# Mode rows in two-byte parts, a later start of gating, and moved norms, taps and restores in a four-layer kernel of long convolutions

## The chip, the cores and the metric

The kernel runs on one core of one Trainium2 chip. A core has TensorE (PE, matrix products), VectorE (DVE), ScalarE (ACT), GpSimd (POOL) and a queue that issues transfers (SP, SyncE); POOL can issue transfers too. Each engine works through its own list of instructions in order and waits on semaphores for the others. The metric is the time of one execution on the device in microseconds, as the median of several runs.

## The reference

Four layers, A, B, A, B, each added to its input. The input x is `q`, 2048 positions by 512 channels.

```python
def A(q, k, v, shift_k, ssm_k, ssm_D):        # q is layernorm(x)
    k_shift = short causal convolution of k with 4 taps per channel
    kv = k_shift * v
    y = irfft(rfft(kv, 4096) * rfft(ssm_k, 4096))[:2048] + kv * ssm_D
    return q * y

def B(u, log_A_real, A_imag, C_real, C_imag, log_dt, D_skip):   # u is layernorm(x)
    dt = exp(log_dt);  A = -exp(log_A_real) + 1j * A_imag;  C = (C_real + 1j * C_imag) * dt
    K = 2 * einsum("dn,dnl->dl", C, exp(A * dt * l)).real       # 128 modes per channel, l = 0..2047
    y = irfft(rfft(K, 4096) * rfft(u, 4096))[:2048]
    return y + u * D_skip

x = q
x = x + A(layernorm(x));  x = x + B(layernorm(x))
x = x + A(layernorm(x));  x = x + B(layernorm(x))
```

In A only the factor `q` depends on x; in B the kernel K does not. So the convolution of A and the spectrum of K are the same in both rounds.

## The kernel before

**Convolutions.** The 512 channels go in 4 quarters of 128, a transform of 4096 points in two steps of matrix products: `fwd_group` multiplies by a table (L171, `pf<-u,wz` or `pf<-kk,wz`) and VectorE transposes the result (L189, L191); `f2_chunk` (L196, `pu<-…,w2`) makes one of 8 chunks of a quarter's spectrum. For a kernel's spectrum (`spectrum_quarter`) four loads `kk` come (L229), POOL adds D to the first tap (L239), and the chunks are copied by ScalarE (`pc`, L247) and stored to `spec` (L248). In `convolution` a chunk is multiplied by the stored spectrum `kab`: ScalarE swaps real and imaginary part (`sw`, L281, L282), VectorE multiplies `vv` (L283), POOL multiplies `sw` (L285) and adds (L286, every third one on VectorE in B). The way back is L295 (`pi<-vv,mm`), a copy (L296), a transpose (`w`, L310) and L316 (`po<-w,w4`); then `finish` takes `po` away.

**Taps of B.** The exponents of the modes are made on four tiles of 128 by 512 (`la`, `ai`, `ph`, `t2`): decay, turns per step, and phase and log magnitude of C. `split` (L359 to L366) parts each into a high and a low four-byte half (`hl`, cast L362 and subtraction L363) and writes both, transposed, to `rows_d`. From there `load_rows` fetches the rows of 32 channels (`raw`, L470), 16 times in all, and VectorE casts them to the matmul's four-byte form (`rw`, L472). Each `rw` gives 10 matmuls against small tables of steps: `mags` (L479, `pm`, 6 of them, then an exponential on ScalarE, L485) and `angles` (L494, `pa`, 4 of them). For an angle VectorE rounds to whole turns (`y`, L498) and a second matmul (L499, table `minus`) subtracts them in the same bank. `waves` takes sine and cosine (L505 to L507), `products` multiplies them on POOL and VectorE (`xye`, L517 to L521), `contract` (L531) sums over the modes, and the taps go to `kdram` (L543), whence `spectrum_quarter(1, q)` loads them as `kk`.

**Gating of A.** `gated(grp)` makes `kv` for 32 channels, 16 groups in all: a load (L624), four multiplies by taps on POOL (L629), a copy on ScalarE (L635), three additions and a product on VectorE (L637, L639), a store (L640). `kv_steps` goes through the groups in three steps each.

**What sets the order.** The code asks for the work in steps, and two generators take turns: `stream` (taps, 64 steps, and B's spectra after each quarter) and `diagonal` (A's spectra in 48 steps, gating, then A's convolution), one step of the first to two of the second; four steps of `diagonal` go ahead of all. A scheduler then puts each engine's list in order by its own estimates; `after(a, b)` gives it an order between two instructions that needs no wait. The first layer follows: `gated_update` loads A's result (`yaq`, L723) and x (L720) and updates x, with statistics; `conv_b(0)` is the second layer, in which the norms `u` of a quarter (`norm`, L798 to L815) run on the engines that `NORM1`, `NORMQ` name; then `gated_update` and `conv_b(1)` for the second round. In the second round x is changed back by `restore` (L818 to L820, 16 additions of `off` on VectorE), asked for at the third quarter's start. Buffers come from named pools; a buffer's `bufs` says how many there are.

Of the kernel before, what the change touches and what calls it, by code (L numbers as in the profile page):

```python
# [11 lines left out]
F16 = mybir.dt.float16  # L12
# [8 lines left out]
NQ = 4  # L21
# [58 lines left out]
def mode_constants():  # L80
    m = np.arange(32)
    n2 = np.concatenate([32 + m, 31 - m])
    tabs = {
        "tt": (np.concatenate([m + 1, 64 * m + 32]), np.repeat([0, 1], 32)),
        "tg1": (n2, 0 * n2),
        "tg2": (64 * m, 0 * m + 1),
    }
    out = {}
    for name, (rate, off) in tabs.items():
        t = np.zeros((2, 2, 16, 2, 16, len(rate)), np.float32)  # L90
        for ch in range(16):
            t[:, 0, ch, :, ch] = rate
            t[:, 1, ch, :, ch] = off
        out[name] = t.reshape(128, 16, len(rate))
    out["minus"] = -np.eye(128, dtype=np.float32)
    return out
# [3 lines left out]
def kernel(ctx: ExitStack, tc: tile.TileContext, out, x_in, kv_in, ssmk_in, ssmd_in,  # L100
# [18 lines left out]
    rows_d = [dram.tile([NQ, 128, 4, 128], F32, name=f"rows_d{k}") for k in range(2)]  # L119
# [23 lines left out]
    psum, swapped, turned, added = {}, [None], [None], [None]  # L143
# [29 lines left out]
    def fwd_group(src, z, c0, n, step, first=None, tag="c1", full=True, early=None):  # L173
        for j in range(0, n, step):
# [12 lines left out]
            if step == 32:  # L187
                for r in range(2):
                    turned[0] = V.transpose(zr[:, :, r], pf[..., r].rearrange("p a x t -> p x a t"))  # L189
# [33 lines left out]
    def spectrum_quarter(which, q, src, pool, zlast, zb, tag):  # L223
# [3 lines left out]
        for g in range(4):  # L227
            kk = pool.tile([128, 512], F32, name="kk", tag="kk", bufs=3 - which)
            nc.sync.dma_start(kk, src[4 * q + g])  # L229
# [12 lines left out]
        for c in range(NCH):  # L242
# [3 lines left out]
            pc = pool.tile([128, CK * 128], F32, name="pc", tag="pc", bufs=2)  # L246
            S.copy(pc, pu.rearrange("p k c -> p (k c)"))  # L247
# [5 lines left out]
    def convolution(which, pools, steps, finish, lag, ahead, nk, ns, nw, inplace, add_dve, zlast=None, late_step=None, first_b=False):  # L253
# [18 lines left out]
        for s in range(-2 * NCH, NS + lag + NCH + 1):  # L272
# [3 lines left out]
            if 0 <= s < NS:  # L276
# [6 lines left out]
                V.tensor_mul(vv, pu, kabs[s][:, 0])  # L283
# [73 lines left out]


    def split(i, v, eng):  # L359
        k, r = divmod(i, 2)  # L360
        hl = nat.tile([128, 2, 4, 128], F32R, name="hl", tag="hl", bufs=4)
        S.copy(hl[:, 0], v)  # L362
        eng.tensor_sub(hl[:, 1], v, hl[:, 0])  # L363
        nc.sync.dma_start(rows_d[k].rearrange("q (h r x) g n -> r (q h) x (g n)", h=2, r=2)[r]
                          .rearrange("a (c p) y -> a c (p y)", p=2),
                          hl.rearrange("p s g n -> p (s g n)").bitcast(F32))  # L366
# [52 lines left out]
    for key, w_, src in (("tg2", 32, tg2_in), ("tg1", 64, tg1_in), ("tt", 64, tt_in)):  # L419
        tabs[key] = gp.tile([128, 16, w_], F32R, name=key)  # L420
# [38 lines left out]

    rows, ms, pks, angs = {}, {}, {}, {}  # L460
# [3 lines left out]
    def load_rows(gi):  # L464
        if gi in rows:
            return
        raw = wk.tile([128, 2, 128], F32, name="raw", tag="raw", bufs=2)
        q, g = divmod(gi, 4)
        for k in range(2):
            nc.sync.dma_start(raw[:, k, :], rows_d[k][q, :, g, :])  # L470
        rows[gi] = wk.tile([128, 2, 128], F32R, name="rw", tag="rw", bufs=2)
        V.tensor_copy(rows[gi], raw)  # L472

    def mags(gi, k, col):
        h, s = divmod(k, 2)
        hs = slice(64 * h, 64 * h + 64)
        pm = pp.tile([128, 512], F32, name="pm", tag="pa", bufs=NPA)
        rhs = tabs["tg2"][hs] if col == 2 else tabs["tg1"][hs, 8 * s:8 * s + 8, :]
        mt = T.matmul(pm, rows[gi][hs, 1, :], rhs, start=True, stop=True)  # L479
# [10 lines left out]
    def angles(gi, k):  # L490
        h, s = divmod(k, 2)
        hs = slice(64 * h, 64 * h + 64)
        pa = pp.tile([128, 512], F32, name="pa", tag="pa", bufs=NPA)
        T.matmul(pa, rows[gi][hs, 0, :], tabs["tt"][hs, 8 * s:8 * s + 8, :], start=True, stop=False,  # L494
# [116 lines left out]
    with ExitStack() as actx:  # L611
# [31 lines left out]
        KV0 = 1  # L643
# [35 lines left out]
        def diagonal():  # L679
            kvs = kv_steps()  # L680
            for q in range(NQ):
                for i, _ in enumerate(spectrum_quarter(0, q, ssmk_in, ap, zlast, ZA, "c1")):
                    if q == 0 and i == 1:
                        for grp in range(KV0):
                            for _ in gated(grp):
                                pass
# [14 lines left out]
            yield from convolution(0, {"conv": ap}, steps_a, finish_a, lag=LAGA, ahead=AHA, nk=NKA, ns=NSA, nw=NWA, inplace=True,  # L701
# [262 lines left out]
```

## Time and profile before

| | us |
|---|---|
| median of 3 runs (739.62 to 749.3) | 739.74 |
| profiled execution, whole | 734.99 |
| profiled execution, span | 733.2 |
| busy in the span: PE, DVE, ACT, POOL | 593.9, 531.1, 486.0, 454.8 |

The profiled execution is 4.75 us below the median; all times of single instructions are from it. Its mean granted TensorE clock is 0.933 of full speed. The stages on its time axis: preparation of the modes to about 45 us, with A's first spectra beside it; taps, spectra and A's convolution to about 422; the first layer's update to 455; the second layer with the last spectra of B to about 595; the third layer to about 616; the fourth to the end. In rows of the timeline the columns are start, length, engine, line, operation, output and inputs, count, and in brackets how long the engine was idle before and what released it; in rows of groups the busy time and the mean duration in ns stand behind the bar, then the idle time ahead of the group.

### The profile page before, as it was taken

Reading aid. Unit: us, or ns where it says so; the run is one execution under the profiler, and the core shown is the slowest. Engines: PE = TensorE matmul, PEld = TensorE weight load, DVE = VectorE, ACT = ScalarE, POOL = GpSimd, SP = SyncE. Lnnn points to the kernel's source line nnn. Section 1 sums busy time; section 2 is a strip of 40 time slices with the busy share of each in tenths; the row PEclk is TensorE's granted clock in tenths of the full one; section 3 lists DMA queues with packets and bytes.
Section 4 is the critical chain, followed back from the end, with each engine's and each line's share of the span. In section 5 each row is a group of like instructions: output and inputs, shape, how many; then the busy total and the mean of one; then the engine's idle time right before and its main releaser. Section 6 shows DMA issues by size and latency. Waiting matters only on the chain. (4 is left out here: it accounts for less than half of the span.)

```text
span 733.2 us, 14282 instructions
## 1 busy us (share of the span) xinstructions
PE 593.9 (81%) x4984; PEld 409.9 (56%) x4984; DVE 531.1 (72%) x961; ACT 486.0 (66%) x882; POOL 454.8 (62%) x473
## 2 busy tenths in 40 slices
PE   1378877698989999969998865899798817799996
PEld 0154554456766776736765454767476503476773
DVE  7857959877385785584574877376597998978775
ACT  4246566577678777776798749677655447768672
POOL 5847969678268595684596620157576612479693
PEclk9997979768999999989999996999999978899999
DMA  9769767774745457636457493567866360178682
GB/s 324 258 227 315 255 209 235 226 249 158 223 125 143 130 127 204 167 107 173 118 149 212 136 335 150 170 181 203 226 192 164 85 172 0 51 209 238 195 244 100
DMA packets 80683, 135.39 MB, mean 185 GB/s; under 512 B 8540, under 2 KB 29412, under 8 KB 79460
## 3 DMA queue, kind: packets, MB, share of 16 engines
q1 hardware_dynamic: 79716, 132.06, 60.3%
q0 software_dynamic: 896, 2.43, 1.2%
q8 instruction: 39, 0.64, 0.4%
q14 instruction: 32, 0.26, 0.1%
HBM read 98.80 MB, written 35.65 MB: 183 GB/s over the span
## 5 line engine op out<-in xcount | busy, mean ns | idle before, releaser
L285 POOL TENSOR_TENSOR sw<-sw,kab 128x512 f32<-128x512 f32 x96 | 124.9, 1305 | 66.3 <-ACT sw L282 61.3
L283 DVE TENSOR_TENSOR vv<-pu,kab 128x512 f32<-128x512 f32 x96 | 65.1, 680 | 64.1 <-ACT sw L282 44.1
L295 PE MATMUL pi<-vv,mm 128*128 128x128 f32 x768 | 105.7, 281 | 6.7 <-DVE vv L283 4.3
L286 POOL TENSOR_TENSOR vv<-vv,sw 128x512 f32<-128x512 f32 x76 | 98.6, 1301 | 14.5 <-DVE vv L283 12.0
L295 PEld LDWEIGHTS pi<-vv,mm 128*128 128x128 f32 x768 | 94.2, 193 | 20.6 <-issue 10.4
L281 ACT ACTIVATE sw<-pu 64x512 f32<-64x512 f32 x96 | 57.1, 595 | 65.7 <-PE pu L196 61.8
L171 PE MATMUL pf<-kk,wz 128*128 128x256 f32 (+1 forms) x176 | 64.7, 624 | 42.1 <-issue 15.2
L517 POOL TENSOR_TENSOR xye<-co,m 128x512 f32<-128x512 f32 x64 | 76.0, 1187 | 36.5 <-ACT co L507 12.5
L629 POOL TENSOR_TENSOR term<-kvt 128x512 f32<-128x512 f32 x64 | 81.5, 1292 | 19.5 <-ACT acc L635 9.8
L196 PEld LDWEIGHTS pu<-zu,w 128*128 128x128 f32 x512 | 63.0, 191 | 42.8 <-DVE vv L283 16.1
L196 PE MATMUL pu<-x,w 128*128 128x128 f32 x512 | 79.6, 302 | 5.9 <-ACT pc L247 2.5
L196 PEld LDWEIGHTS pu<-x,w 128*128 128x128 f32 x512 | 70.7, 209 | 21.9 <-issue 7.5
L196 PE MATMUL pu<-zu,w 128*128 128x128 f32 x512 | 72.8, 284 | 10.7 <-DVE vv L283 9.6
L171 PE MATMUL pf<-u,wz 128*128 128x256 f32 (+2 forms) x280 | 76.4, 485 | 3.0 <-DVE zu L189 1.2
L247 ACT COPY pc<-pu 128x512 f32<-128x512 f32 x64 | 37.2, 587 | 45.3 <-PE pu L196 22.6
L485 ACT ACTIVATE m<-pm 128x512 f32<-128x512 f32 x96 | 53.4, 607 | 18.5 <-PE pm L479 15.1
L316 PE MATMUL po<-w,w 128*64 128x512 f32 x192 | 53.9, 637 | 13.8 <-DVE w L310 12.0
L171 PEld LDWEIGHTS pf<-kk,wz 128*128 128x128 f32 (+1 forms) x176 | 30.1, 222 | 58.2 <-issue 29.3
L505 ACT ACTIVATE co<-pa 128x512 f32<-128x512 f32 x64 | 38.4, 600 | 30.2 <-PE pa L499 29.8
L282 ACT COPY sw<-pu 64x512 f32<-64x512 f32 x96 | 55.5, 578 | 1.1
L518 DVE TENSOR_TENSOR xye<-pa,m 128x512 f32<-128x512 f32 x64 | 43.7, 683 | 13.8 <-ACT pa L506 7.3
L479 PE MATMUL pm<-tg,rw 64*128 64x512 f32 x96 | 43.7, 517 | 10.5 <-DVE xye L519 8.3
(137 smaller groups left out, 1147.3 us busy)
## 6 DMA issues: line engine op xcount, KB each, us to landing
kab<-spec SPq DMA_DIRECT2D x188, 256.0 KB, 4.3
spec<-pc SPq DMA_DIRECT2D x64, 256.0 KB, 2.3
kvt<-kv_in SPq DMA_DIRECT2D x16, 624.0 KB, 5.3
yaq<-ya_d SPq DMA_DIRECT2D x5, 1024.0 KB, 7.5
kk<-ssmk_in SPq DMA_DIRECT2D x16, 256.0 KB, 5.1
kv_d<-un SPq DMA_DIRECT2D x16, 256.0 KB, 4.1
xt<-x_in SPq DMA_DIRECT2D x16, 256.0 KB, 2.9
kdram<-ks SPq DMA_DIRECT2D x64, 64.0 KB, 2.9
```

The source lines that it names most:

```text
L171: yield T.matmul(o, w, rhs, start=True, stop=True)
L196: ins = T.matmul(pu[:, i, :], w2[:, c * CK + i, :], z[:, :, c * CK + i, :], start=True, stop=True)
L281: S.mul(sw[0:64], pu[64:128], -1.0)
L282: swapped[0] = S.copy(sw[64:128], pu[0:64])
L283: V.tensor_mul(vv, pu, kabs[s][:, 0])
L285: (V if last else G).tensor_mul(sw, sw, kabs[s][:, 1])
L286: (V if last or s % add_dve == add_dve - 1 else G).tensor_add(vv, vv, sw)
L295: i1s[t] = T.matmul(pi[:, i, :], mm[:, c * CK + i, :], vvs[t][:, i, :], start=True, stop=True)
L316: ins = T.matmul(po[64 * a:64 * a + 64], w4, ws[g][:, :, 16 * a:16 * a + 16, :].rearrange("p x t r -> p t x r"), start=True, stop=True, ti ...
L485: i = S.activation(m, pm.rearrange("p (c i) -> p c i", c=16 if col == 2 else 8), AF.Exp)
L517: G.tensor_mul(xye[:, 0, :, 32:96], co[:, :, 1:65], m[:, :, 32:96])
L629: G.tensor_mul(term, kvt[:, 3 - j:19 - j, :], tap(j))
```

## The change

1. **Mode rows.** `split` makes three two-byte parts, each the rounded rest of what is left, and a fourth part of zeros, so that the 128 partitions of `rw` hold 2 halves of the channels, 2 kinds of rows, 8 channels and 4 parts. That is one more cast on ScalarE and one more subtraction per tile (POOL for `la` and `ai`, VectorE for `ph` and `t2`). `rows_d` holds bf16, `load_rows` loads straight into `rw` (3 buffers), the cast is gone. The tables `tt`, `tg1`, `tg2` are bf16. L479 and L494 become two-byte matmuls over 64 rows (128 for the second kind of magnitudes) with the same 512 columns. The subtraction of whole turns (L499) keeps its four-byte form.
2. **Gating.** No group is done ahead (`KV0` 1 to 0); the first four steps of A's spectra go without gating (`KS`), and what is left of the gating at the end of the spectra is done beside the first 7 steps of A's convolution instead of before it.
3. **Last quarter of B's spectra.** Its four loads `kk` are issued by POOL instead of SP; `pc` has 4 buffers instead of 2 for B's spectra.
4. **Norms.** In the second layer the norms of the second quarter are ordered behind the last copy of B's spectra.
5. **Restores** are ordered each behind the product asked for just before it (`multiplied`), instead of all behind the last transpose asked for at the quarter's start.

```diff
-    rows_d = [dram.tile([NQ, 128, 4, 128], F32, name=f"rows_d{k}") for k in range(2)]
+    rows_d = [dram.tile([NQ, 2, 128, 4, 128], BF16, name=f"rows_d{k}") for k in range(2)]
...
-            nc.sync.dma_start(kk, src[4 * q + g])
+            (G if which and q == NQ - 1 else nc.sync).dma_start(kk, src[4 * q + g])
...
-            pc = pool.tile([128, CK * 128], F32, name="pc", tag="pc", bufs=2)
-            S.copy(pc, pu.rearrange("p k c -> p (k c)"))
+            pc = pool.tile([128, CK * 128], F32, name="pc", tag="pc", bufs=2 + 2 * which)
+            last_pc[0] = S.copy(pc, pu.rearrange("p k c -> p (k c)"))
...
-                V.tensor_mul(vv, pu, kabs[s][:, 0])
+                multiplied[0] = V.tensor_mul(vv, pu, kabs[s][:, 0])
...
+    pieces = []
+    for i in range(4):
+        parts = nat.tile([128, 4, 4, 128], BF16, name=f"parts{i}")
+        G.memset(parts[:, 3], 0.0)
+        pieces.append(parts)
...
-        hl = nat.tile([128, 2, 4, 128], F32R, name="hl", tag="hl", bufs=4)
-        S.copy(hl[:, 0], v)
-        eng.tensor_sub(hl[:, 1], v, hl[:, 0])
-        nc.sync.dma_start(rows_d[k].rearrange("q (h r x) g n -> r (q h) x (g n)", h=2, r=2)[r]
-                          .rearrange("a (c p) y -> a c (p y)", p=2),
-                          hl.rearrange("p s g n -> p (s g n)").bitcast(F32))
+        parts = pieces[i]
+        rest = nat.tile([128, 4, 128], F32, name="rest", tag="rest", bufs=2)
+        S.copy(parts[:, 0], v)
+        eng.tensor_sub(rest, v, parts[:, 0])
+        S.copy(parts[:, 1], rest)
+        eng.tensor_sub(parts[:, 2], rest, parts[:, 1])
+        nc.sync.dma_start(rows_d[k].rearrange("q h (s r c p) g n -> r (q h s) c (p g n)", s=2, r=2, p=4)[r],
+                          parts.rearrange("p s g n -> p (s g n)"))
...
-        raw = wk.tile([128, 2, 128], F32, name="raw", tag="raw", bufs=2)
+        rows[gi] = wk.tile([128, 2, 2, 128], BF16, name="rw", tag="rw", bufs=NR)
         q, g = divmod(gi, 4)
         for k in range(2):
-            nc.sync.dma_start(raw[:, k, :], rows_d[k][q, :, g, :])
-        rows[gi] = wk.tile([128, 2, 128], F32R, name="rw", tag="rw", bufs=2)
-        V.tensor_copy(rows[gi], raw)
+            nc.sync.dma_start(rows[gi][:, k], rows_d[k][q, :, :, g, :].rearrange("h x n -> x h n"))
...
-        rhs = tabs["tg2"][hs] if col == 2 else tabs["tg1"][hs, 8 * s:8 * s + 8, :]
-        mt = T.matmul(pm, rows[gi][hs, 1, :], rhs, start=True, stop=True)
+        T.matmul(pm, rows[gi][hs, 1, h, :], tabs["tg2" if col == 2 else "tg1"][hs], start=True, stop=True)
...
-        T.matmul(pa, rows[gi][hs, 0, :], tabs["tt"][hs, 8 * s:8 * s + 8, :], start=True, stop=False,
+        T.matmul(pa, rows[gi][hs, 0, h, :], tabs["tt"][hs], start=True, stop=False,
...
-        KV0 = 1
+        KV0 = 0
+        KS = 4
...
-                    next(kvs, 0)
+                    if 12 * q + i >= KS:
+                        next(kvs, 0)
...
+            stage_banks(4, 0)
+            main = convolution(0, {"conv": ap}, steps_a, finish_a, lag=LAGA, ahead=AHA, nk=NKA, ns=NSA, nw=NWA, inplace=True,
+                               add_dve=ADA, zlast=zlast)
+            for _ in range(NCH - 1):
+                next(kvs, 0)
+                next(main)
+                yield
             for _ in kvs:
                 yield
-            stage_banks(4, 0)
...
+                    elif rnd == 0 and q == 1:
+                        after(i, last_pc[0])
...
-                after(V.tensor_scalar(x[:, t, :], x[:, t, :], off[:, t:t + 1], None, op0=ALU.add), turned_first[0])
+                after(V.tensor_scalar(x[:, t, :], x[:, t, :], off[:, t:t + 1], None, op0=ALU.add), multiplied[0])
```

How this moves the lists. SP at the start of the taps; before, the rows are loaded (L470) behind two stores and two loads of gating (L640, L624):

```order
L364 DMA rows_d_98<-hl 8x16x1024
L364 DMA rows_d_99<-hl 8x16x1024
L640 DMA kv_d_82<-un 128x512
L624 DMA kvt<-kv_in 128x1248
L229 DMA kk<-ssmk_in 128x512
L640 DMA kv_d_83<-un 128x512
L624 DMA kvt<-kv_in 128x1248
L226 DMA dr<-ssmd_in 1x128
L470 DMA raw<-rows_d_98 128x128
```

The same place after; the loads of rows are L480:

```order
L374 DMA rows_d_98<-parts_141 16x8x2048
L228 DMA dr<-ssmd_in 1x128
L374 DMA rows_d_99<-parts_147 16x8x2048
L231 DMA kk<-ssmk_in 128x512
L480 DMA rw<-rows_d_98 128x2x128
L480 DMA rw<-rows_d_99 128x2x128
```

The gating's transfers no longer stand between the writing of the rows and their reading.

SP at the end of A's convolution; before, with the last loads of taps (`kdram_77` to `kdram_80`) among the loads of A's result (`yaq`):

```order
L229 DMA kk<-kdram_76 128x512
L229 DMA kk<-kdram_77 128x512
L723 DMA yaq<-ya_d 128x1536
L723 DMA yaq<-ya_d 128x512
L226 DMA dr<-dsk_in 1x128
L723 DMA yaq<-ya_d 128x1536
L723 DMA yaq<-ya_d 128x512
L543 DMA kdram_80<-ks 32x4x128 x4
L229 DMA kk<-kdram_78 128x512
L723 DMA yaq<-ya_d 128x1536
```

And after, where the last quarter's taps are loaded from POOL's list:

```order
L231 DMA kk<-kdram_76 128x512
L733 DMA yaq<-ya_d 128x1536
L733 DMA yaq<-ya_d 128x512
L733 DMA yaq<-ya_d 128x1536
L228 DMA dr<-dsk_in 1x128
L733 DMA yaq<-ya_d 128x512
L733 DMA yaq<-ya_d 128x1536
L733 DMA yaq<-ya_d 128x512
L733 DMA yaq<-ya_d 128x2048
```

The loads of A's result stand together, ahead of the last store of taps.

VectorE at the start of the fourth layer's second half; before, 14 restores (L820) in one piece ahead of the first product (L283):

```order
L189 STREAM_TRANSPOSE zu<-pf 128x512 x10
L820 TENSOR_SCALAR x<-x,off 128x512 x14
L283 TENSOR_TENSOR vv<-pu,kab 128x512
L820 TENSOR_SCALAR x<-x,off 128x512 x2
L283 TENSOR_TENSOR vv<-pu,kab 128x512
L189 STREAM_TRANSPOSE zu<-pf 128x512 x2
```

And after, with the product now L285 and the restore L832:

```order
L191 STREAM_TRANSPOSE zu<-pf 128x512 x10
L285 TENSOR_TENSOR vv<-pu,kab 128x512
L832 TENSOR_SCALAR x<-x,off 128x512 x2
L285 TENSOR_TENSOR vv<-pu,kab 128x512
L832 TENSOR_SCALAR x<-x,off 128x512 x2
L285 TENSOR_TENSOR vv<-pu,kab 128x512
L832 TENSOR_SCALAR x<-x,off 128x512 x2
L191 STREAM_TRANSPOSE zu<-pf 128x512 x2
```

Two restores follow each product.

More of the change, by code (lines that the diff above doesn't have):

```diff
@@ L11 @@
 F32R = mybir.dt.float32r
-F16 = mybir.dt.float16
+BF16 = mybir.dt.bfloat16
 I32 = mybir.dt.int32
@@ L83, in mode_constants @@
     tabs = {
-        "tt": (np.concatenate([m + 1, 64 * m + 32]), np.repeat([0, 1], 32)),
-        "tg1": (n2, 0 * n2),
-        "tg2": (64 * m, 0 * m + 1),
+        "tt": (8, np.concatenate([m + 1, 64 * m + 32]), np.repeat([0, 1], 32)),
+        "tg1": (8, n2, 0 * n2),
+        "tg2": (16, 64 * m, 0 * m + 1),
     }
     out = {}
[L89 to L94, printed above, removed]
+    for name, (chans, rate, off) in tabs.items():
+        t = np.zeros((2, 2, 8, 4, chans, len(rate)), np.float32)
+        for s in range(2):
+            for c in range(8):
+                for r, factors in enumerate((rate, off)):
+                    t[s, r, c, :3, (8 * s + c) % chans] = factors
+        out[name] = t.reshape(128, chans, len(rate))
     out["minus"] = -np.eye(128, dtype=np.float32)
@@ L188, in fwd_group @@
                 for r in range(2):
[L189 removed]
+                    V.transpose(zr[:, :, r], pf[..., r].rearrange("p a x t -> p x a t"))
             else:
@@ L418 @@
     tabs = {}
-    for key, w_, src in (("tg2", 32, tg2_in), ("tg1", 64, tg1_in), ("tt", 64, tt_in)):
-        tabs[key] = gp.tile([128, 16, w_], F32R, name=key)
+    for key, c_, w_, src in (("tg2", 16, 32, tg2_in), ("tg1", 8, 64, tg1_in), ("tt", 8, 64, tt_in)):
+        tabs[key] = gp.tile([128, c_, w_], BF16, name=key)
         G.dma_start(tabs[key], src)
@@ L457 @@
         factors.append(xye)
+    NR = 3
     rows, ms, pks, angs = {}, {}, {}, {}
@@ L682, in diagonal @@
                 for i, _ in enumerate(spectrum_quarter(0, q, ssmk_in, ap, zlast, ZA, "c1")):
[L683 to L686, printed above, removed]
                     if q == 0 and i < 4:
@@ L697, in diagonal @@
                     yield
+            stage_banks(4, 0)
[5 more added lines that the diff above has]
+                yield
             for _ in kvs:
                 yield
-            stage_banks(4, 0)
-            yield from convolution(0, {"conv": ap}, steps_a, finish_a, lag=LAGA, ahead=AHA, nk=NKA, ns=NSA, nw=NWA, inplace=True,
-                                   add_dve=ADA, zlast=zlast)
+            yield from main
         RT = 1
@@ L825, in start @@
         def start(c):
-            if rnd == 1 and q == 2 and c == 0:
-                turned_first[0] = turned[0]
             if rnd == 1 and q == 2:
```

8 lines of the change are left out of this document (4 added, 4 removed).

## The prediction

> **What bounds the kernel now.** I read the chain of work that ended last first, then the busy times of the engines by stage, then the groups of the matmuls that change, and the timeline at the places that the change touches. The chain, by engine and by line:
>
> ```profile
> PE 20%; DVE 8%; DMA 6%; ACT 3%; issue 3%; POOL 2%; SPq 0%; DVEq 0%; POOLq 0%; ACTq 0%
> PE pu L196 7%; PE pf L171 6%; PE pi L295 5%; PE po L316 3%; DMA kab<-spec 2%; DMA yaq<-ya_d 2%; DVE x L745 1%; DVE vv L283 1%; DVE x L820 1%; DMA kk<-kdram 1%; DVE st L865 1%; DVE st L753 1%; ACT sw L281 1%; DVE w L310 1%; POOL sw L285 1%
> ```
>
> TensorE leads, but the chain names less than half of the span and no line of the modes, so the stages have to be looked at one by one. Windows of the trace (start:end and length, busy time and count of each engine, the granted clock, the DMA engines' share and GB/s):
>
> ```profile
> 45.00:180.00 135.00, 109.14 (x1007) 68.26 (x1010) 106.57 (x200) 85.28 (x150) 103.99 (x111) 0.82 0.72 235
> 180.00:422.00 242.00, 219.89 (x2391) 156.83 (x2381) 156.92 (x254) 188.26 (x325) 158.14 (x162) 0.99 0.55 154
> 640.00:734.00 94.00, 84.94 (x568) 60.54 (x567) 68.23 (x90) 57.83 (x104) 67.34 (x60) 0.97 0.69 196
> 140.00:160.00 20.00, 15.31 (x109) 9.81 (x110) 15.79 (x32) 11.51 (x21) 13.65 (x14) 0.68 0.80 259
> 420.00:440.00 20.00, 13.82 (x140) 11.12 (x140) 15.66 (x29) 9.91 (x18) 4.88 (x7) 1.00 1.00 331
> ```
>
> From 180 to 422 TensorE works 91% of the time at a clock of 0.99, so work taken off it there shortens the stage until ScalarE, at 188 of 242 us, is next. From 45 to 180 it works 81% at 0.82, with VectorE and POOL at 78%: nothing alone carries that stage. At 420 to 440 the DMA engines are full.
>
> **Two-byte mode rows, 180 to 422.** The change turns the magnitude matmuls (L479) and the first angle matmuls (L494) from four-byte into two-byte operands, and leaves the second angle matmul (L499) as it is. By form, in the windows 180:422 (first two rows) and 45:180 (last two):
>
> ```profile
> L479 PE MATMUL pm<-tg,rw 64*128 64x512 f32 x60 | 24.5, 470 | 3.0 <-ACT m L485 1.7 <-DVE xye L519 1.1
> L494 PE MATMUL pa<-tt,rw 64*128 64x512 f32 x40 | 18.5, 482 | 6.4 <-DVE xye L519 6.3
> ...
> L479 PE MATMUL pm<-tg,rw 64*128 64x512 f32 x36 | 19.2, 594 | 7.5 <-DVE xye L519 7.3
> L494 PE MATMUL pa<-tt,rw 64*128 64x512 f32 x24 | 13.2, 629 | 1.5 <-ACT m L485 1.0 <-DVE xye L519 0.5
> ```
>
> A duration includes the way through the array; what a matmul takes from the engine is the distance to the next start:
>
> ```profile
> 203.82 0.49 PE L494 MATMUL pa<-tt,rw 64*128 64x512 f32 x1
> 204.24 0.49 PE L499 MATMUL pa<-y,minus 128*128 128x512 f32 x1
> 204.67 0.49 PE L494 MATMUL pa<-tt,rw 64*128 64x512 f32 x1
> 205.09 1.99 PE L171 MATMUL pf<-u,wz 128*128 128x256 f32 x8
> ```
>
> That is 0.42 to 0.43 us for 512 columns. No two-byte matmul is in this trace. One end is that it costs no less (0 saved), the other that time goes with the bytes of a column (0.21 saved, an estimate from these rows); 100 matmuls then give 0 to 21 us. I take the larger price, since nothing in these rows but the columns sets the spacing, and of the 21 us 0.6, thus 13: TensorE idles 22 us of this stage already, waiting for ScalarE and VectorE, whose work stays, and each gap opens further when its matmuls get shorter. The extra weight loads of the two-byte form lie beside the matmuls (PEld 157 us against PE 220). The Trainium skill, "TensorE: Matmul & The Clock Gate", section "Back-to-back issue gap", gives about 216 ns for 512 two-byte columns at full clock; no run here shows it yet, and by it the saving is the same 0.21.
>
> **The casts.** The same rows are cast on VectorE for the four-byte matmuls; after the change they arrive ready.
>
> ```profile
> L472 DVE CAST rw<-raw 128x256 fp32r<-128x256 f32 x16 | 17.4, 1090 | 0.0
> ...
> 319.91 6.21 DVE L472 CAST rw<-raw 128x256 fp32r<-128x256 f32 x1
> ...
> 324.66 1.30 POOL L286 TENSOR_TENSOR vv<-vv,sw 128x512 f32<-128x512 f32 x1
> ...
> 328.01 1.98 PE L316 MATMUL po<-w,w 128*64 128x512 f32 x4 [6.37 <-DVE w L310]
> ```
>
> One of the 16 took 6.21 us and ended just when POOL's unbroken work ended (324.66 + 1.30), and TensorE stood 6.37 us for it. I take 5 of it (0 to 6.4); the other casts are within VectorE's slack.
>
> **45 to 180.** Here 60 matmuls lose 0.21 us at full clock, at 0.82 thus 0.26: 15 us of TensorE. Against that about two gating groups move in from ahead of 45, since gating now starts with the fifth spectrum step: 8 multiplies on POOL. Their price is in the POOL row below, 8.71/7 = 1.24 us, thus 10 us more on POOL, at 104 of 135 us already. From +15 (TensorE decides) to −5 (half of POOL's work shows); I take 3, nearer to the losing end because no engine leads. The tail of gating beside the first seven convolution steps adds no work, only order.
>
> **Start.** The rows' way to the taps (SP's queue, and the engines around it):
>
> ```profile
> 25.04 0.62 ACT L362 CAST hl<-ph 128x512 fp32r<-128x512 f32 x1 [0.45 <-DVE ph L414]
> 25.69 0.69 DVE L363 TENSOR_TENSOR hl<-ph,hl 128x512 fp32r<-128x512 f32 x1 [0.68 <-ACT hl L362]
> ...
> 26.41 1.25 SPq L364 DMA_DIRECT2D rows_d<-hl  x2
> 26.74 8.71 POOL L629 TENSOR_TENSOR term<-kvt 128x512 f32<-128x512 f32 x7 [2.29 <-ACT acc L635]
> ...
> 34.47 0.38 SPq L640 DMA_DIRECT2D kv_d<-un  x1
> ...
> 35.98 3.63 SPq L470 DMA_DIRECT2D raw<-rows_d  x4
> ...
> 44.11 1.60 PE L479 MATMUL pm<-tg,rw 64*128 64x512 f32 x3
> ```
>
> The rows are written at 26.4 to 27.7, but read at 36.0, behind the stores and loads of gating on SP. Without these the read can follow the write: about 8 us earlier. A third part costs each of the two last splits one more cast (0.62) and subtraction (0.69), together 2.6 us on the way. The reading in 256-byte pieces and the zeroing of the fourth part on POOL cost something too, the latter hidden, as POOL waits there (2.29 us in its row). From +8 to −3 (these extras with nothing gained, because the tables or the banks come last); I take 3, as POOL still has the first additions of spectra to make.
>
> **From the last spectra to the second layer.** Queue of SP, then ScalarE and the waits of TensorE from 422 to 482:
>
> ```profile
> 423.45 2.06 SPq L229 DMA_DIRECT2D kk<-kdram  x2
> ...
> 431.93 3.54 SPq L723 DMA_DIRECT2D yaq<-ya_d  x3
> 435.57 20.23 SPq L248 DMA_DIRECT2D spec<-pc  x8
> 455.90 0.89 SPq L229 DMA_DIRECT2D kk<-kdram  x2
> ...
> 455.52 9.34 ACT L808 ACTIVATE u<-x,nb,rs 128x128 f32<-128x128 f32 x24
> ...
> 475.62 6.27 ACT L808 ACTIVATE u<-x,nb,rs 128x128 f32<-128x128 f32 x16
> 481.91 0.59 ACT L281 ACTIVATE sw<-pu 64x512 f32<-64x512 f32 x1
> ...
> PE pu L196 <- ACT pc L247: 10.2, 3, 9.6
> ```
>
> On SP the loads of A's result stand behind loads of taps that wait for their stores, and the last taps behind the stores of spectra, until 455.9. Both chains come apart when the four last taps go through POOL's queue, which has little to do there (4.88 us in 420:440). Also, 16 norms of 0.39 us (6.2) leave the place ahead of the last copies of spectra, for which TensorE waits 9.6 us at once; but they then stand, with the 16 of 475.62, ahead of the first product at 481.91. Gain 0 (the DMA engines are full at 1.00, and the norms only change places) to 10 (the waits of TensorE); I take 5, the middle. POOL's queue, if it came late, would hold what is behind the loads there, the additions of D.
>
> **Restores.** In the last round 14 restores stand in one piece ahead of the first product; after, they follow the products two by two.
>
> ```profile
> 626.92 8.65 DVE L820 TENSOR_SCALAR x<-x,off 128x512 f32<-128x512 f32 x14
> ...
> 636.09 1.89 DVE L820 TENSOR_SCALAR x<-x,off 128x512 f32<-128x512 f32 x2
> ...
> 636.23 2.08 PE L196 MATMUL pu<-zu,w 128*128 128x128 f32 x8 [4.45 <-DVE vv L283]
> ...
> 636.32 1.38 POOL L286 TENSOR_TENSOR vv<-vv,sw 128x512 f32<-128x512 f32 x1 [3.01 <-DVE vv L283]
> ```
>
> TensorE stands 4.45 us behind them. All of it is the upper bound; the lower is −4: the 16 × 0.6 = 9.6 us then fall into a stretch where VectorE has 27% free (640 to 734: 68 of 94), and half may show. I take 2, as three quarters of the wait go and some of the spread comes back. A rule speaks against it: the Trainium skill, "GPSIMD Engine Reference", section "1. Specifications", says that POOL shares its SBUF interfaces with VectorE, with contention against VectorE's instructions in a two-port mode. The 6.21-us cast agrees; by this rule restores among POOL's products would wait for POOL's pauses, the rival R4.
>
> **Sum.** 13 + 5 + 3 + 3 + 5 + 2 = 31. The profiled execution took 734.99 us, so 704; the median of the runs, 739.74, lies 4.75 above it, so **709**.
>
> **Rivals.** Two per cent is about what a measurement of this kernel can tell from no change: 725 and 754.5 are the bounds.
> - R1: the stages fall onto the next wait, ScalarE's exponentials and VectorE's products, and shorter matmuls only lengthen TensorE's pauses. For it: the 6.3 us before L494 that wait for products. Against: 91% busy. Both terms of the matmuls are 0, the other 15 stay: 735 − 15 + 4.75 = 725. Chance 0.17, half of it beyond the bound.
> - R2: two-byte matmuls cost no less than four-byte ones, so the change does not do what it is made of. The same sum, 725. Against it speaks only that the spacing of the rows follows the columns. Chance 0.05.
> - R3, slower: the clock. With thinner work TensorE from 45 to 422 is granted less. Its work at full clock is 109.14 × 0.82 + 219.89 × 0.99 = 307 us; less 34 it is 273, which at the 0.68 of 140:160 takes 402 instead of 377: +25, and with the gains at start, transition and restores (10) 755. It decides from a clock of 0.70 down (273/387). Against it: 420:440 has less TensorE work (13.8 of 20) than 140:160 (15.3) and a clock of 1.00. The Trainium skill, "TensorE: Matmul & The Clock Gate", Part 1 on the clock gate, states that an idle window of some 3.4 us halves the clock; the trace's 0.82 and 0.99 bear it out only as far as the busier stage has the higher clock. Chance 0.07.
> - R4: the restores wait for POOL as that cast did. One such wait of 6 us, on a path that now lies ahead of L295, turns +2 into −6: 709 + 8 = 717. Against it: the 16 restores before ran at 8.65/14 = 0.6 us, in a stretch where POOL was idle at least 3.01 us. Chance 0.15.
>
> The forecast has 0.56. Faster by over 2%: 0.55 of it, 0.13 of R4, 0.06 of R1 and 0.02 of R2, 0.76; within: 0.17; slower 0.07. The range: low end 696, where the matmuls of 180 to 422 give 21 and those of 45 to 180 give 8 (−13); high end 733, R1 with the transition's 5 and the start's 3 at zero. It leaves out R3 and a little at both ends.
>
> **What would show it.** Right: the changed matmuls 0.21 to 0.22 us apart at full clock, the stage from 180 some 13 to 20 us shorter, no VectorE instruction of 6 us in it; the first magnitude matmul near 36 instead of 44; A's result loaded straight after its store; the first product of the last quarters 8 us earlier. Wrong: equal spacing (R2); the same stage with more idle time of TensorE behind L485 or L518 (R1); a clock under 0.75 from 45 on (R3); restores of over 1 us (R4).

## The result, and the profile after

The changed kernel takes 727.44 us (median of 4 runs, 725.52 to 731.89), the kernel before 739.68 (4 runs): a ratio of 0.9866, 95% interval 0.9818 to 0.9914. A second set gave 0.9872 (0.9826 to 0.9918). That is 12 us where 31 were forecast: inside the range given, but two fifths of the step, and within 2%. The ratios are of the faster executions alone, the medians of all.

The windows of the profile after, as shown for the kernel before (busy time and count of PE, PEld, DVE, ACT, POOL, granted clock, DMA share, GB/s):

```profile
45.00:180.00 135.00, 102.17 (x972) 60.17 (x971) 101.42 (x191) 81.46 (x143) 101.78 (x105) 0.85 0.70 225
180.00:422.00 242.00, 221.57 (x2381) 154.62 (x2380) 154.75 (x257) 189.16 (x329) 171.29 (x177) 0.96 0.61 171
```

From 180 to 422 TensorE is as busy as before, though its matmuls got shorter. Counted as busy time multiplied by clock, it has 5 us less work there (221.57 x 0.96 = 213 instead of 219.89 x 0.99 = 218) and 3 less in 45 to 180 (102.17 x 0.85 = 87 instead of 109.14 x 0.82 = 89). The changed matmuls in 180:422, then in 45:180, by form:

```profile
L486 PE MATMUL pm<-tg,rw 64*128 64x512 bf16 x40 | 14.0, 386 | 1.7 <-ACT m L492 1.3
L501 PE MATMUL pa<-tt,rw 64*128 64x512 bf16 x41 | 13.5, 394 | 2.2 <-DVE xye L526 1.8
...
L501 PE MATMUL pa<-tt,rw 64*128 64x512 bf16 x23 | 8.5, 409 | 7.6 <-DVE xye L526 6.0 <-ACT m L492 1.5
L486 PE MATMUL pm<-tg,rw 64*128 64x512 bf16 x22 | 8.0, 432 | 2.7 <-ACT m L492 2.6
```

The magnitudes take 386 ns where the four-byte form had 470: 0.08 us less, not 0.21. How long the first half of the kernel takes is read from the views of three tiles, the magnitudes, the sums over modes and A's result, by their first and last start (here x number: shortest, median, longest in ns, first to last start in us). The kernel before, then after:

```profile
L479 PE MATMUL pm<-tg,rw x96: 383/492/1412, 44.1 to 396.0; 64*128 64x512 f32 x96
L531 PE MATMUL pk<-xye x2048: 216/219/317, 74.2 to 426.1; 128*32 128x64 f32 x187
L677 SPq DMA_DIRECT2D ya_d<-ya x16: 359/376/1164, 278.4 to 423.0; - x16
```

```profile
L486 PE MATMUL pm<-tg,rw x96: 372/387/628, 41.0 to 396.8; 64*128 64x512 bf16 x64, 128*128 128x512 bf16 x32
L538 PE MATMUL pk<-xye x2048: 216/219/317, 73.0 to 437.1; 128*32 128x64 f32 x187
L685 SPq DMA_DIRECT2D ya_d<-ya x16: 360/366/435, 273.1 to 419.4; - x16
```

The chain of work that ended last in the kernel after, by engine and line:

```profile
PE 31%; DVE 9%; ACT 9%; issue 5%; POOL 3%; DMA 3%; SPq 0%; DVEq 0%; POOLq 0%; ACTq 0%
PE pu L198 9%; PE pf L173 7%; PE po L318 6%; PE pi L297 6%; DMA kab<-spec 3%; ACT u L818 2%; DVE x L755 1%; POOL sw L287 1%; DVE w L312 1%; PE pk L538 1%; DVE x L832 1%; DVE vv L285 1%; ACT sw L283 1%; PE pm L486 1%; ACT sw L284 1%
```

The loads of A's result (`yaq`, 2% before) and of the taps (`kk`, 1%) are gone from this list; the restores (`DVE x`, now L832) are still there with 1%.

The taps start 3.1 us earlier, and what is called the stretch below, from there to the last store of A's result, is 378.4 us instead of 378.9: the forecast had taken 21 us from it. The last sum over modes even starts 11 us later, 437.1 instead of 426.1: in the new order the last taps come behind the end of A's convolution. The transition, from the first factor of the update (`ut`, 431.2 before, 429.8 after) to the first product of the second layer (484.2, 478.5), is 48.7 us instead of 53.0; from there to the last factor of the second update (607.1, 601.9) the length changes by less than 1 us, and the rest takes 2.1 us longer. Together that is 3.1 us between the two profiles.

The medians differ by more. The profiled execution of before was a lucky one, 4.75 us under its median, that of after an unlucky one, 4.45 over. Their mean granted clocks are 0.933 and 0.921; in 29 runs of the kernel before, made beside the first experiments, the median clock is 0.920, and a higher clock goes with a shorter time, 4.2 us per 0.01 (correlation -0.67). That the clock makes the difference is likely, but not shown. So the lengths of stages are taken from the profiles here, and effects on the whole time from ratios of many runs.

### The profile page after: what moved, and what is told of

Same layout as the page of the kernel before. It is cut to its first block, busy times and chain, and to the rows that moved or that the text cites. A ratio compares the mean times of both kernels' runs of the same rounds, so it can differ in the third digit from the quotient of the medians.

```text
span 730.1 us, 14266 instructions
## 1 busy us (share of the span) xinstructions
PE 587.1 (80%) x4984; PEld 398.4 (55%) x4984; DVE 525.5 (72%) x947; ACT 487.2 (67%) x886; POOL 461.7 (63%) x483
## 4 chain that ended last, share of the span: by engine, by line
PE 31%; DVE 9%; ACT 9%; issue 5%; POOL 3%; DMA 3%; SPq 0%; DVEq 0%; POOLq 0%; ACTq 0%
PE pu L198 9%; PE pf L173 7%; PE po L318 6%; PE pi L297 6%; DMA kab<-spec 3%; ACT u L818 2%; DVE x L755 1%; POOL sw L287 1%; DVE w L312 1%; PE pk L538 1%; DVE x L832 1%; DVE vv L285 1%; ACT sw L283 1%; PE pm L486 1%; ACT sw L284 1%
## 5 line engine op out<-in xcount | busy, mean ns | idle before, releaser
L285 DVE TENSOR_TENSOR vv<-pu,kab 128x512 f32<-128x512 f32 x96 | 65.1, 681 | 73.9 <-ACT sw L284 40.7
L297 PEld LDWEIGHTS pi<-vv,mm 128*128 128x128 f32 x768 | 95.8, 195 | 21.6 <-issue 14.2
L283 ACT ACTIVATE sw<-pu 64x512 f32<-64x512 f32 x96 | 57.1, 595 | 59.7 <-PE pu L198 56.4
L173 PE MATMUL pf<-kk,wz 128*128 128x256 f32 (+1 forms) x176 | 61.9, 599 | 39.3 <-issue 16.0
L318 PE MATMUL po<-w,w 128*64 128x512 f32 x192 | 57.2, 683 | 9.5 <-DVE w L312 8.2
L538 PEld LDWEIGHTS pk<-xye 128*32 128x32 f32 x2048 | 36.8, 116 | 37.0 <-issue 18.4
L538 PE MATMUL pk<-xye 128*32 128x64 f32 x2048 | 51.6, 235 | 6.3 <-DVE ks L548 4.0
```

Of the source, the lines that this page charges most:

```text
L173: yield T.matmul(o, w, rhs, start=True, stop=True)
L283: S.mul(sw[0:64], pu[64:128], -1.0)
L285: multiplied[0] = V.tensor_mul(vv, pu, kabs[s][:, 0])
L297: i1s[t] = T.matmul(pi[:, i, :], mm[:, c * CK + i, :], vvs[t][:, i, :], start=True, stop=True)
L318: ins = T.matmul(po[64 * a:64 * a + 64], w4, ws[g][:, :, 16 * a:16 * a + 16, :].rearrange("p x t r -> p t x r"), start=True, stop=True, ti ...
L538: T.matmul(pk[32 * i4:32 * i4 + 32, 2 * k + i, :], xye[:, r, 4 * i + i4, 64:96], xye[:, r, 4 * i + i4, 0:64], start=r == 0, stop=r == 1, t ...
```

## Experiments

Six of the runs are marked "held". The scheduler makes each engine's list anew from its own estimates, so that changing one part reorders the rest. In a held kernel each instruction of an engine is ordered, without a wait, behind the one ahead of it in the other kernel's list:

```diff
+    for i in seq:
+        ins = traced[i]
+        if ins.engine in last:
+            tc.add_manual_dep(ins, last[ins.engine].name,
+                              mybir.DependencyInfo(mybir.DependencyClass.NoSync, mybir.DependencyReason.DATA), reason="held order")
+        last[ins.engine] = ins
```

All measured ratios are to the kernel before on the same chip, with the 95% interval; the chips differ from one set of runs to the next. Products are counted from 0 over the 96 of the whole kernel: the first layer's convolution has 0 to 31, the second layer 32 to 63, the fourth 64 to 95.

**The whole change again.**

> The whole change once more, for a second profile and a narrower interval. In the first profile the second layer lost 9.7 us between its products 32 and 48 (from 5.7 us ahead of the kernel before to 3.9 behind), while the DMA engines were full at 500 to 520 us. If that loss is built into the new order: about 727 us again, and the products 40 to 48 at 501 to 536 us in this profile too. If it was an accident of that execution: product 48 at 527 us or earlier (5 us ahead of before) and a profiled execution near 726 us.

0.9872. The lengths repeat: the stretch is 378.2 us (40.7 to 418.9) beside 378.4. Products 40 and 48 stood at 494.7 and 527.9 us (495.4 and 528.8 in the first profile, 502.3 and 531.7 before). The loss of 9.7 us from which the expectation sets out is not there: it held product 49 of the changed kernel against product 48 of the one before. In the first profile the lead falls from 5.7 us at product 32 to 2.9 at product 48 and is 5.5 again at product 62.

**One part at a time, order made anew.** The parts are those of the diff above, put alone into the kernel before.

> Kernel before with the two-byte mode rows alone (three parts, bf16 tables, direct loads, no casts). Theory 1, the price: the stage of the taps is bound by TensorE, and a changed matmul saves 0.10 us instead of 0.21 because its weight load shows; 16 us of TensorE less at full clock, and the cast's stall of 5: 739.7 - 13 to 20 = 720 to 727. Theory 2, the next wait: TensorE's work is no longer what ends the stage, so only the cast's stall and the start count: 732 to 736. Theory 3, gating: the rows alone give more than the whole change, because the later gating costs: below 725.

> Kernel before with the later start of gating alone (no group ahead, none in the first four steps of A's spectra, the rest beside the first seven steps of A's convolution). Theory 3: A's convolution begins later (its first product was 5.8 us later in the whole change) and the end of the taps with it: 743 to 748. Theories 1 and 2: gating has slack either way and the start gains up to 3: 736 to 740.

> Kernel before with the last quarter's loads on POOL's queue, four buffers for the copies of B's spectra, and the second quarter's norms behind the last copy. By the term of the prediction (5 us at the transition): 734 to 736, with the first product of the second layer 4 to 6 us earlier than 484.2. If the DMA engines' full stretch or the norms take it back: 738.5 to 741, with that product within 2 us of 484.

> Kernel before with the restores alone behind the products. By the prediction's term: 2 us faster, 736 to 738. By the two profiles of the whole change, in which the 9 us that the first products of the last half gained were gone 12 products later: 738 to 741, with single restores of 1 us and more while POOL multiplies.

Rows 0.9985 (0.9947 to 1.0023), gating 1.003 (1.000 to 1.006), last quarter with norms 0.9928 (0.988 to 0.9976), restores 0.9998 (0.9956 to 1.0041). The rows alone shorten the stretch to 369.3 us (55.6 to 424.9), but begin it 11.5 us later. In their profile (VectorE, SP's queue, TensorE):

```profile
42.66 0.67 DVE L372 TENSOR_TENSOR parts<-rest,parts 128x512 bf16<-128x512 f32 x1
...
46.26 0.89 SPq L373 DMA_DIRECT2D rows_d<-parts  x1
...
49.54 5.49 SPq L479 DMA_DIRECT2D rw<-rows_d  x4
...
55.56 0.71 PE L485 MATMUL pm<-tg,rw 128*128 128x512 bf16 x3 [2.65 <-DMA rw<-rows_d]
```

The third part, which the last split makes in turns of ScalarE and VectorE, is done at 43.3; its store waits on SP behind transfers of gating and of A's spectra until 46.3, the load of the rows until 49.5. The later gating alone starts the taps at 38.0 instead, and makes the stretch 10 us longer (389.1):

```profile
L479 PE MATMUL pm<-tg,rw x96: 385/492/1412, 38.0 to 400.0; 64*128 64x512 f32 x96
L678 SPq DMA_DIRECT2D ya_d<-ya x16: 359/377/546, 286.7 to 427.1; - x16
```

So alone each of these two parts gives back what it gains.

> Kernel before with the last quarter's loads on POOL's queue and four copy buffers, the norms as before. If the loads carry the gain of that part (ratio 0.993 with the norms): 733 to 737. If the norms carried it: 738.5 to 741.

The edit is the last quarter without the norms:

```diff
-            nc.sync.dma_start(kk, src[4 * q + g])
+            (G if which and q == NQ - 1 else nc.sync).dma_start(kk, src[4 * q + g])
...
-            pc = pool.tile([128, CK * 128], F32, name="pc", tag="pc", bufs=2)
+            pc = pool.tile([128, CK * 128], F32, name="pc", tag="pc", bufs=2 + 2 * which)
```

1.001 (0.9965 to 1.0055); the medians of all runs, 736.40 and 741.79 for the kernel before beside them, would give 0.993, so whether the time changes is open. In its profile the transition is 5.2 us shorter than before, with the norms (the run above) 3.3. So the loads shorten the transition, and in that profile the new order ahead of it (first factor at 436.4 instead of 431.2) took that away; what the norms add is not settled.

> The changed kernel with the mode rows in two four-byte halves and their casts as before; all other parts stay. From the two parts run alone: the later gating starts the taps at 38 us and makes the stretch from the first magnitude matmul to the last store of A's result 10 us longer (389), and the rows take 9.6 of it back when they are there. If the parts add up so: 389 to 391 us for that stretch, and 733 to 738 in all, 6 to 10 slower than the whole change. If the rows bring nothing in company either (as alone, ratio 0.9985): 727 to 730.

1.0182 (1.0135 to 1.0229), and not in the way expected: the stretch is 368.7 us, but the last sum over modes starts at 463.6 instead of 426.1. The scheduler put A's convolution first and the taps late, so that this run compares two orders and says little about the rows.

**How much the stage owes to TensorE.** The magnitude matmuls get half of their columns, and the exponential reads these twice (that edit is not shown), so that the magnitudes of half of the steps are left out:

```diff
-        mt = T.matmul(pm, rows[gi][hs, 1, :], rhs, start=True, stop=True)
+        n = 8 if col == 2 else 4
+        T.matmul(pm[:, 0:256], rows[gi][hs, 1, :], rhs[:, 0:n, :], start=True, stop=True)
```

In the kernel after, the same edit is at L486.

> Kernel before with the 96 magnitude matmuls (L479) at half their columns, 256 instead of 512, the exponential reading these 256 twice; the taps are then wrong for half of the steps. All counts, waits and the work of the other engines stay, and TensorE has 96 x 0.21 = 20 us less. Theory 1 (TensorE bounds the taps' stage): from the first magnitude matmul to the last store of A's result 378.9 us becomes 362 to 367, and the time 724 to 728. Theory 2 (the next wait): that stretch stays at 374 to 381 and the time at 735 to 741. The distance of two such matmuls tells besides what a four-byte matmul is made of: 0.21 if time goes with the columns alone, over 0.25 if a weight load is part of it.

> The changed kernel with its 96 magnitude matmuls (L486) at 256 instead of 512 columns, read twice, the taps wrong for half of the steps as in the run beside it. If the 0.32 us of a two-byte matmul of 512 columns are its columns alone, the distance falls to 0.16; if they are 0.21 for the columns and 0.11 for a weight load that does not lie beside the matmul ahead, to 0.21. Theory 1: 96 x 0.11 = 10 us of TensorE less, 718 to 722. Theory 2: 726 to 730.

> As half_before (96 magnitude matmuls at 256 columns, 20 us less of TensorE), but every engine's list keeps the order of the kernel before, instead of the order that the scheduler makes anew for shorter matmuls. Theory order (half_before was 1.4% slower because the scheduler put the taps later, its last sum over modes at 464 us instead of 426): with the order held the stretch from the first magnitude matmul to the last store of A's result is no longer than the 378.9 us of before, 366 to 378, and the time 727 to 738. Theory clock (thinner TensorE work is granted less, as the mean clock of 0.891 against 0.933 says): slower than before even so, 742 to 750.

> As half_after (10 us less of TensorE than the whole change), with every engine's list in the order of the whole change. half_after was about 1% slower than the whole change. Theory order: 722 to 728, at or below the whole change. Theory clock: 732 to 738, with a mean clock near 0.90.

With the order made anew, both kernels with less work came out slower than those that they were made from: 1.0139 (1.009 to 1.0187) against 1, and 0.9978 (0.994 to 1.0016) against 0.9872; the last sum over modes of the first stands at 464.1. In the old orders it is 0.9962 (0.9914 to 1.0011), and 0.989 (0.9833 to 0.9946), the same as the whole change. So the same work in another order differs by 1.8% (1.0139 to 0.9962). The stretch of half_before_held is 375.4 us (45.4 to 420.8) instead of 378.9. And these kernels tell what a matmul is made of. TensorE of half_before_held, of half_after_held, and of the changed kernel; each first row starts one matmul, the next row's start ends its time on the engine:

```profile
223.88 0.38 PE L480 MATMUL pm<-tg,rw 64*128 64x256 f32 x1
224.19 1.16 PE L196 MATMUL pu<-x,w 128*128 128x128 f32 x8
```

```profile
226.50 0.28 PE L486 MATMUL pm<-tg,rw 64*128 64x256 bf16 x1
226.71 1.16 PE L297 MATMUL pi<-vv,mm 128*128 128x128 f32 x8
```

```profile
232.39 0.39 PE L486 MATMUL pm<-tg,rw 64*128 64x512 bf16 x1
232.71 0.54 PE L538 MATMUL pk<-xye 128*32 128x64 f32 x22
```

A four-byte matmul takes 0.42 us with 512 columns (rows in the prediction) and 0.31 with 256, a two-byte one 0.32 and 0.21. In both forms 256 columns cost 0.11; the rest, 0.20 and 0.10, does not depend on the columns. The weight loads show what it is, in the kernel before and then in the changed one:

```profile
203.82 0.18 PEld L494 LDWEIGHTS pa<-tt,rw 64*128 64x128 f32 x1 [0.33 <-issue]
204.24 0.19 PEld L499 LDWEIGHTS pa<-y,minus 128*128 128x128 f32 x1 [0.24 <-issue]
```

```profile
232.39 0.09 PEld L486 LDWEIGHTS <-rw 64*128 64x128 bf16 x1
232.71 0.37 PEld L538 LDWEIGHTS pk<-xye 128*32 128x32 f32 x22 [0.23 <-issue]
```

The load takes 0.18 us in the four-byte form and 0.09 in the two-byte one, and the next load then comes only 0.24 and 0.23 us later, when the columns are through: at these places load and columns follow each other. It is not so everywhere. Two 64-row matmuls can also go side by side, as here in the changed kernel, two in the 0.39 us of one:

```profile
189.97 0.39 PE L486 MATMUL pm<-tg,rw 64*128 64x512 bf16 x2
```

So 0.10 us is what the narrower form saves at a matmul that stands alone. The Trainium skill, "TensorE: Matmul & The Clock Gate", section "LDWEIGHTS (loading the stationary operand)", gives the time of a load in ns as the columns of the weights divided by 1.2, whatever the rows, which makes an estimate of 107 for 128 columns. The two-byte loads agree with it roughly, with a median of 93; the four-byte ones do not, with 183, and there the measurement decides.

**The rows, their cast and their price in a held order.** First the rows alone in the order of before, with four buffers for them; then the four-byte rows without their cast, in that order:

```diff
-        raw = wk.tile([128, 2, 128], F32, name="raw", tag="raw", bufs=2)
         q, g = divmod(gi, 4)
+        rows[gi] = wk.tile([128, 2, 128], F32R, name="rw", tag="rw", bufs=4)
         for k in range(2):
-            nc.sync.dma_start(raw[:, k, :], rows_d[k][q, :, g, :])
-        rows[gi] = wk.tile([128, 2, 128], F32R, name="rw", tag="rw", bufs=2)
-        V.tensor_copy(rows[gi], raw)
+            nc.sync.dma_start(rows[gi][:, k, :].bitcast(F32), rows_d[k][q, :, g, :])
```

> Kernel before with the two-byte mode rows alone, four buffers for them, and every engine's list in the order of the kernel before (the third part's cast and subtraction right behind the second's). Theory order: the delay of the rows that the scheduler's new order gave (first magnitude matmul at 55.6 instead of 44.1) shrinks to the two casts and subtractions, 46 to 49; the stretch to the last store of A's result loses the 16 us of matmuls by half and the cast's stall, 365 to 371; in all 728 to 734. Theory next wait: the stretch stays above 373 and the time at 736 to 741.

> Kernel before with its four-byte mode rows loaded straight into the matmul's buffer (four of them) instead of through the 16 casts on VectorE; the halves are written already rounded, so nothing else changes, and every engine's list keeps the order of before. Theory stall: the 7.5 us that the two-byte rows gave with that order were the cast's stall of 6.4, not the shorter matmuls: 732 to 735, and the products of A's convolution from the 17th to the 21st on 5 to 7 us earlier, nothing before. Theory price: the shorter matmuls gave it: 737 to 740, with another instruction late in the cast's place.

0.9899 (0.9836 to 0.9961) and 0.9917 (0.9873 to 0.9962): the same, as are the medians, 730.07 and 729.40 us. Starts of products of A's convolution on VectorE, in us:

| product | before | cast free, held | two-byte rows, held |
|---|---|---|---|
| 8 | 260.07 | 257.49 | 260.23 |
| 16 | 309.75 | 307.52 | 308.29 |
| 20 | 336.24 | 327.85 | 328.51 |
| 28 | 386.13 | 378.79 | 377.42 |

Both gain 6.2 us between products 16 and 20, where the 6.21-us cast stood. In the kernel without casts (rows below) VectorE goes on there, and no instruction takes over the stall:

```profile
318.89 0.69 DVE L283 TENSOR_TENSOR vv<-pu,kab 128x512 f32<-128x512 f32 x1 [1.14 <-ACT sw L282]
319.50 1.24 DVE L310 STREAM_TRANSPOSE w<-x 128x1024 f32<-128x1024 f32 x1
```

The shorter matmuls take the stretch from 371.5 us (cast free) to 365.0 (two-byte rows), and the later rows give 5.4 of these 6.5 back at the start:

```profile
L477 PE MATMUL pm<-tg,rw x96: 385/492/1412, 44.3 to 390.1; 64*128 64x512 f32 x96
L675 SPq DMA_DIRECT2D ya_d<-ya x16: 359/376/554, 276.7 to 415.8; - x16
...
L485 PE MATMUL pm<-tg,rw x94: 372/387/631, 49.7 to 388.5; 64*128 64x512 bf16 x64, 128*128 128x512 bf16 x30
L683 SPq DMA_DIRECT2D ya_d<-ya x16: 359/377/2097, 279.2 to 414.7; - x16
```

Over the whole run TensorE is busy 9.6 us less (596.3 to 586.7) at nearly the same clock (0.925 and 0.923). Both runs that follow have the four-byte rows without cast, the first in the order of the whole change.

> The whole change with four-byte mode rows in two halves, loaded without a cast, and every engine's list in the order of the whole change (the third part's casts and subtractions gone). The 160 matmuls take 0.42 instead of 0.32 us: 16 us more of TensorE. Theory stall (the rows' gain was the cast alone): 725 to 731, like the whole change (727 to 730). Theory price (the shorter matmuls carry the gain in company): 736 to 745, with the stretch from the first magnitude matmul to the last store of A's result at 386 or more instead of 378.

> The same with gating from the third step, in the order of that kernel (723.1, ratio 0.978, with two-byte rows). Theory stall: 720 to 726. Theory price: 731 to 740. If TensorE matters more where other waits are fewer: slower than 723 by more than the run beside it is slower than the whole change.

In the order of the whole change the median is 741.17 us of 12 runs (733.31 to 753.54), for which no ratio is given. With gating from the third step it is 0.9948 (0.9906 to 0.9989), 737.84 us against 723.06 for the two-byte rows, which ran on another chip. In company the two-byte form is worth 12 to 15 us by these medians. By the profile of rows4_held 4.5 of them are the start (first magnitude matmul at 45.5), which the matmuls do not explain, and 9.9 the stretch (388.3 us); TensorE is busy 599.4 us there against 587.1 after, at the same clock of 0.921. That order was made for short matmuls, the order of before for long ones, so the worth of the form probably lies between. Shorter still gains nothing: half_after_held has 10 us less of TensorE by the count (96 x 0.11), 5.7 by its busy time (581.4), and stayed at the whole change's time. TensorE's longest wait in total is there for ScalarE's exponentials, 9.9 us where the whole change has 7.6 (view of waits, 45 to 425: total, times, longest):

```profile
PE pm L486 <- ACT m L493: 9.9, 15, 2.0
```

**Gating's start, and the restores in company.** One number is changed, to 2 and to 0; then `KS = 2` with the restores in one piece again.

```diff
-        KS = 4
+        KS = 2
```

```diff
-                after(V.tensor_scalar(x[:, t, :], x[:, t, :], off[:, t:t + 1], None, op0=ALU.add), multiplied[0])
+                after(V.tensor_scalar(x[:, t, :], x[:, t, :], off[:, t:t + 1], None, op0=ALU.add), turned_first[0])
```

> The whole change with gating from the third step of A's spectra instead of the fifth. If the later gating costs in the stage what it gives at the start (-6 us and +10 us, run alone): the first magnitude matmul up to 3 us later than 41, the stretch to the last store of A's result 3 to 5 us shorter than 378, in all 724 to 729. If the order that the scheduler makes decides more than the amount of work moved: anywhere from 720 to 745, with no such trade in the profile.

> The whole change with gating from the first step of A's spectra (still no group ahead). Theory trade (work moved from the start into the stage): from KS = 4 to 2 the first magnitude matmul went from 41.0 to 43.4 and the stretch to the last store of A's result from 378 to 366; here 45 to 50 and 355 to 366, and 718 to 728 in all. Theory order: no such line through the three, the stretch above 370 again, 728 to 740.

> The whole change with gating from the third step and the restores in one piece as before, in nearly the same order elsewhere. Alone the restores moved nothing (ratio 0.9998), since each waited for POOL's products. If that holds in company: 721 to 725, like the run with the restores behind the products (723.1). If they gave something in company: 725 to 729.

KS = 2 gave 0.9781 (0.9716 to 0.9847), 723.06 us, the fastest order found. KS = 0 gave 1.0054 (1.0009 to 1.0098), though its median, 738.19, lies under the 741.79 beside it: no gain can be read from it. The stretch is 378.4 us with 4, 366.8 with 2 and 385.5 with 0: it does not follow the amount of work moved. With the restores back: 0.9826 (0.9771 to 0.988), not to be told from 0.9781. So they are neutral in company too. Why, the profiles show: first the kernel before (VectorE, behind its 14 restores), then the whole change (VectorE, POOL, and the view of the tile `off`):

```profile
635.49 0.68 DVE L283 TENSOR_TENSOR vv<-pu,kab 128x512 f32<-128x512 f32 x1
```

```profile
623.70 0.69 DVE L285 TENSOR_TENSOR vv<-pu,kab 128x512 f32<-128x512 f32 x1 [1.09 <-ACT sw L284]
624.31 2.40 DVE L832 TENSOR_SCALAR x<-x,off 128x512 f32<-128x512 f32 x2
626.64 0.68 DVE L285 TENSOR_TENSOR vv<-pu,kab 128x512 f32<-128x512 f32 x1
```

```profile
623.75 2.68 POOL L287 TENSOR_TENSOR sw<-sw,kab 128x512 f32<-128x512 f32 x2 [7.89 <-ACT sw L284]
```

```profile
L832 DVE TENSOR_SCALAR x<-x,off x16: 459/898/1534, 624.3 to 646.1; 128x512 f32<-128x512 f32 x16
```

The two restores take 2.40 us and end just behind POOL's pair (626.43); the median is 898 ns where it was 478. Product 64, the first of the fourth layer, came 11.8 us earlier than before, product 76 (661.1 instead of 665.8) only 4.7, which is about what the layer had started ahead (5.2).

## Why the prediction was wrong, step by step

- **Two-byte rows, 180 to 422 (13) and the 15 us of TensorE in 45 to 180.** This step failed by its price. "Time goes with the bytes of a column" is not so: the columns cost the same in both forms, and only the weight load is halved, 0.10 us of 0.42 where 0.21 was taken. Nor do the changed matmuls stand the 216 ns apart that the prediction quotes: 0.32 us is measured, and the measurement decides. 160 matmuls give at most 16 us of TensorE, not 21 + 15; its busy time fell by 9.6 us in the order of before and 12.3 in that of after. Of these 6.5 and 9.9 reach the stretch, so the share taken, 0.6, was if anything low and the price twice too high. The rows of before held the answer in reach: the weight loads of 0.18 us, which the prediction put beside the matmuls by their busy sum, without looking at what stood between two starts.
- **The cast's stall (5).** Right: 6.2 us, located and removed alone.
- **Gating (inside the 3 us of 45 to 180, bound -5).** This step failed too, and by more. The stretch is 10 us longer with the later gating alone, and about 13 longer in company (378.4 beside the 365.0 of the two-byte rows in the order of before). The part of it that is POOL's added work cannot be told from the new order; KS = 2 takes 11.6 us off the stretch again with half as many steps kept free.
- **Start (3).** 3.1, but that is luck. Two larger terms stand against each other, and they do not give it: the third part costs 5.4 us in a held order instead of 2.6, the absent gating gives 6.1 in an order of its own. What makes up the rest is not known.
- **Transition (5).** 4.3 in the profile; the loads alone give 5.2 there. (The row at 481.91 is ScalarE's swap; the first product is at 484.22.)
- **Restores (2).** 0: R4, the wait for POOL, is what the rows show, without the loss of 6 that it was priced at. The product that comes earlier is the first of the whole layer, not of its last quarters.
- **The clock's carry (4.75).** It is no step that failed: it brings the forecast from the profile back to the median, 739.74 - 31 = 709.

Of the rivals, R1 (the next wait) accounts for what TensorE saved and the stretch did not get, and it fits half_after_held, which gained nothing more. R2 is refuted by the 0.32 us, though it is right for the columns. R3 fails: the clock is 0.96 instead of 0.99 in 180:422, but 0.85 instead of 0.82 in 45:180. In the sum of the chances R1 stands with 0.06 where half of its 0.17 is 0.085, which changes no choice.

So the gains found add up to 6 (cast), 7 to 10 (rows), 4 (transition) and 3 (start), 20 to 23 us, and 10 to 13 us of the stretch go back to the later gating and the order that the scheduler made for it. That leaves 7 to 13, where the medians show 12. Which of the moves in that order cost the time was not tried.

## What to carry to other kernels

Split a matmul's spacing into columns and weight load before pricing a narrower type: two lengths of the same matmul give both. Where a scheduler sets the order, test a part with the order held; a part that is tested in a new order measures that order too, here up to 1.8% for the same work. Number the instructions that are compared between two profiles in both of them: one product off made a loss of 9.7 us that was none. And look at the clock of two profiled executions before comparing their whole times.

## What was not expected of the hardware

A four-byte matmul in this form costs no more per column than a two-byte one (0.11 us per 256 in both). One VectorE instruction of 128x256 stood 6.2 us while POOL worked without a break, and restores of 0.48 us take 0.90 beside POOL's products. The Trainium skill, "GPSIMD Engine Reference", section "1. Specifications", says that POOL shares its SBUF interfaces with VectorE, with contention against VectorE's instructions in a two-port mode or with two SBUF inputs. These two rows agree with it; in which mode the cast and the restores ran, no run here shows. And the kernel half_before, with less work for TensorE, had a median clock of 0.898 where the kernel before had 0.919 on that chip; whether the thinner work or the new order lowered it was not tried.
